# Softmax rows left unnormalised for the first six pairs of heads, and the output scaled by transposed reciprocals

## The chip, the cores and the metric

The kernel runs on one core of one Trainium2 chip. The metric is the device time in microseconds of one execution. TensorE (PE in the rows, PEld its weight loads), VectorE (DVE), ScalarE (ACT) and GpSimd (POOL) run side by side, each through its own list of instructions in order. SyncE (SP) issues the DMAs.

## The reference

Three stages follow one another: an attention with a threshold, a mixture of neighbouring tokens with a squared ReLU and a gate ("moe"), and a gated convolution ("moe2").

```
# 8 batches, 8 heads, 576 tokens, 64 per head
scores = q @ k.T / 8
thresh = max(scores, axis=-1) - tau
scores = where(scores >= thresh, scores, -1e9)
attn = exp(scores - max(scores))
attn = attn / (sum(attn) + 1e-9)
x = heads joined(attn @ v)                                # 8 x 576 x 512
xk = mu_k*x + (1-mu_k)*x_prev;  xr = mu_r*x + (1-mu_r)*x_prev
k = relu(xk @ w_k);  v = (k*k) @ w_v;  x = sigmoid(xr @ w_r) * v
gate = sigmoid(causal conv of 5 taps over x);  out = (gate * (x @ w_val)) @ w_out
```

## The kernel before

The attention goes through 32 pairs of heads (four pairs to a batch). A pair is nine chunks: chunks 0 to 7 are 128 query rows of one of the two heads in turn, and chunk 8 is the last 64 rows of both. The rows shown below and the prediction count pairs from the first to the thirty-second, nine chunks each.

One chunk passes through the engines so: TensorE forms the scores `s` in PSUM from `qkh` and its small remainder `kl` (four matmuls of 288 columns; eight in chunk 8; L409); VectorE takes their minimum (L419; the scores carry a minus sign); GpSimd adds tau to it (L422); ScalarE writes the exponentials into `p` (L432); VectorE multiplies them with the mask and sums the row into a column of the tile `sm` (L436); the sum is guarded with 1e-9 (L441, on GpSimd for the first 15 chunks, on VectorE after them) and inverted on VectorE (L446); GpSimd multiplies the 128x576 tile `p` with it (L449); TensorE transposes `p` in blocks of 128x128 into a PSUM bank `g` (L466), ScalarE copies these into `pt` (L477, L480, L485, L488). After chunks 3 and 8 TensorE multiplies `pt` with `v` (L515, L518) into a bank, and ScalarE copies that half of the pair's output into `x` (L525), whose rows are the two heads' 64 outputs and whose columns are tokens. Each pair also needs its inputs cast and split (`qkh` L356, L360 on ScalarE, remainders `kl` L364 on VectorE and L370 on GpSimd).

While the first pairs run, the float64 weights w_k and w_v come in as bits and are turned into a high and a low part, 16 pieces of 128x512 (tiles `wst` and `stage`): L264, L274, L304 on ScalarE, L267, L270 on VectorE, L277 on GpSimd, and the low part L307 on VectorE or GpSimd.

When the first batch's four pairs have left their `x`, the products of the moe stage begin (L551, 464 tokens a block, ten blocks, 192 matmuls of w_k and w_v to a block). They are mixed into the rest of the attention on TensorE. After the attention come the products with w_r, w_val and w_out, 1440 matmuls.

PSUM has eight banks. The scores hold two double banks, and a third (`s3`) for the first S3_CHUNKS chunks, if the chunk's number calls for it; after that the third's two banks join `g0` and `g1` as `g2` and `g3`, which transposes, outputs and products share.

The order on each engine isn't that of the code. Each step is recorded with an engine, a due time (its priority) and the buffers that it takes and frees (`acq`, `rel`); a planner then plays them through with estimated durations and emits them in the order it finds. Constants such as EARLY, MOE_LAG (how long after its batch a moe block is due) or MIX_AT shift those due times. An operation given as `{dve: .., pool: ..}` goes to whichever engine the planner finds free, as the low parts of weights do.

Of the kernel before, what the change touches and what calls it, by code (L numbers as in the profile page):

```python
# [8 lines left out]
F32 = mybir.dt.float32  # L9
# [5 lines left out]
ALU = mybir.AluOpType  # L15
# [10 lines left out]
PAD, TW = 4, 464  # L26
# [27 lines left out]
class Plan:  # L54
# [90 lines left out]

EARLY, QK_EARLY, T_LATE, EV_EARLY, AV_LATE = 0.7408, 0.3765, -0.2385, 2.6476, 0.0528
S3_CHUNKS = 48
MOE_LAG = 0.6411  # L150
MOE_STEP = 0.8064
KSTAGE = 4
KBUFS, XKBUFS = 10, 4
CVB = 3
GATES = {"a": 1, "b": 3}
XRS = {"a": 1, "b": 1}
MIX_EARLY, SIDE_EARLY = 1.1121, -0.2697
W_KEY, W_STEP = -0.5451, 2.6541
V_KEY, V_STEP = 1.365, -0.2017
R_AHEAD = 0  # L160
HOP = 240.0
VAL_LAG, OUT_LAG = 2.3457, 3.4035
LATE2, LOAD2, MIX2, CONV_LAG, THR_EARLY = -0.2908, 11.9577, 6.0432, 11.1059, 3.4422
MIX_AT = 332.7791
GUARD_POOL = 15
OUT_FETCH = 8.1497
# [6 lines left out]
def body(ctx, tc, qka, qkb, vp, w_k, w_v, w_r, w_val, w_out, conv_w, par, out):  # L173
    nc = tc.nc
    ctx.enter_context(tc.manual_schedule())
    plan = Plan()
    op = plan.op

    def dma(nbytes, fn, deps=(), prio=0.0, acq=(), rel=()):

        return op("dma", max(480, nbytes / 360), fn, deps, prio, acq, rel, lat=2000)
    tokens = plan.tokens
# [10 lines left out]
    ident = par_t[:, 0:128]  # L193
# [8 lines left out]
                            op0=ALU.mult, op1=ALU.add)  # L202
# [9 lines left out]
    g_s, tau_t = gs[:, 0:1], gs[:, 2:3]  # L212


    XBUFS, RAWS = 8, 2
# [27 lines left out]
    tokens.update(raw=RAWS, qk=4, kla=2, klb=2, v=2, p=3, pt=1, sm=4, s=2, s3=1, g0=1, g1=1,  # L243
                  x=XBUFS, xk=XKBUFS, xf=2, kh=0, cwst=KSTAGE, k2=2, vo=2, mm=2, cstage=1)
    BANKS = tuple(f"g{i}" for i in range(8))
    tokens.update({x: 0 for x in BANKS[2:]})
# [3 lines left out]
    by = {"dve": nc.vector, "pool": nc.gpsimd}  # L250
# [82 lines left out]
    x_t, x_done, x_kept = {}, {}, {}  # L333
    qk_t, kl_t, qk_done = {}, {}, {}
    v_t, v_done = {}, {}
    s_t, p_t, pt_t, sm_t, av_t, tps, tr_op, av_op = {}, {}, {}, {}, {}, {}, {}, {}

    def chain(kind, o):
        last[kind] = o
        return o  # L340
# [48 lines left out]
    def chunk(g):  # L389

        pi, c = seq[g]
        b, pp = pairs[pi]
        j, head = divmod(c, 2)
        at = g * PACE
        both = c == 8
        s_tok = "s3" if g < S3_CHUNKS and g % 3 == 2 else "s"


# [14 lines left out]
        o = op("pe", dur, lambda: qk(0), deps, at - QK_EARLY, acq=(s_tok,))  # L413
        o = chain("qk", op("pe", dur, lambda: qk(1), (o,), at - QK_EARLY, rel=("qk", "qk", "kla", "klb") if c == 8 else ()))
# [76 lines left out]
        o = op("pe", 440 * slow, lambda: tr((g, 0), [(k0 + i * 128, 128) for i in range(4)]), (nm, last.get("t")), lt,  # L491
               acq=(BANKS, "pt") if c in (0, 4) else (BANKS,))
# [5 lines left out]
        if head or c == 8:  # L498
            o = op("pe", 115, lambda: tr((g, 1), [(512, 128 if c < 8 else 64)]), (o,), lt, acq=(BANKS,), rel=("p",))
# [5 lines left out]
        if c in (3, 8):  # L505
            half = c // 8
            n = 256 + 64 * half

            def av():
                pt, ptl = pt_t[pi, half]  # L510
                v = v_t[pi]
                acc = av_t[pi, half] = bank(av_op[pi, half])
                for kc in range(4):
                    for h in range(2):
                        nc.tensor.matmul(acc[h * 64:h * 64 + 64, 0:n],  # L515
                                         lhsT=v[:, kc * 128 + h * 64:kc * 128 + h * 64 + 64],
                                         rhs=pt[:, h, kc, 0:n], start=(kc == 0), stop=False)
# [15 lines left out]
            chain("xe", x_done[b, pp])  # L533
            if half:
# [3 lines left out]
    half_evs = []  # L538

# [209 lines left out]
    def after_first():  # L749
# [5 lines left out]
               rel=BANKS[4:] + ("mm", "mm"))  # L755
# [213 lines left out]
```

## Time and profile before

| | before |
|---|---|
| median of 3 runs | 1294.17 us (1291.86 to 1294.76) |
| the profiled execution | 1293.29 us |
| its span, first to last instruction | 1291.2 us |
| busy: PE, DVE, ACT, POOL | 95%, 74%, 65%, 56% of the span |
| mean granted TensorE clock | 0.989 |

The shares are means over a start in which the attention runs alone, a long middle in which moe products fill TensorE, and an end of products only. 2.1 us of the profiled execution lie outside its span.

### The profile page before, as it was taken

What the parts mean: (1) busy time and instruction counts of PE and PEld (TensorE: products, weight loads), DVE (VectorE), ACT (ScalarE), POOL (GpSimd) and SP (SyncE); (2) the same over time, 40 slices, a digit from 0 to 9 for tenths busy, and PEclk for the clock granted to TensorE, in tenths of its full rate; (3) what the DMA queues carried; (4) which work ended last, traced back from release to release, by engine and by line L of the source; (5) the groups of instructions that cost most, each with busy time, mean ns of one, the idle gap of its engine ahead of it and who ended that gap; (6) DMA issues with size and microseconds to landing.
All of it is one profiled execution on the core that took longest, in us unless ns stands there. A gap on an engine that the chain in (4) does not pass through costs nothing.

```text
span 1291.2 us, 21070 instructions
## 1 busy us (share of the span) xinstructions
PE 1232.2 (95%) x7104; PEld 1041.5 (81%) x7104; DVE 959.2 (74%) x2086; ACT 835.4 (65%) x1608; POOL 724.9 (56%) x953
## 2 busy tenths in 40 slices
PE   5776999999999999999999999999999999999998
PEld 4555778887888887888888888888888888888897
DVE  7999998798888889779799697872433996665520
ACT  7877877777677667577687675662543876554432
POOL 6988766667665666547567456441203854553341
PEclk9889999999999999999999999999999999999999
DMA  7343232342322343223333212105105432230011
GB/s 243 124 129 114 93 99 88 107 138 92 130 83 80 115 124 113 82 85 118 115 105 111 82 61 74 54 11 190 53 15 193 139 118 89 92 110 36 30 48 70
DMA packets 51339, 127.57 MB, mean 99 GB/s; under 512 B 8608, under 2 KB 26144, under 8 KB 50464
## 3 DMA queue, kind: packets, MB, share of 16 engines
q1 hardware_dynamic: 51232, 126.23, 29.3%
q8 instruction: 57, 0.93, 0.3%
q14 instruction: 50, 0.41, 0.1%
HBM read 91.48 MB, written 34.73 MB: 98 GB/s over the span
## 4 chain that ended last, share of the span: by engine, by line
PE 70%; DVE 10%; ACT 7%; POOL 5%; issue 4%; DMA 4%; SPq 0%; DVEq 0%; POOLq 0%; ACTq 0%
PE g L551 43%; PE s L409 9%; PE g L515 8%; PE g L466 7%; PE g L518 3%; POOL p L449 2%; ACT p L432 1%; DVE sm L419 1%; DVE p L436 1%; DVE g L856 1%; POOL qkh L370 1%; ACT pt L477 1%; POOL sm L422 1%; DVE xf L608 1%; DMA xt<-x_d 1%
## 5 line engine op out<-in xcount | busy, mean ns | idle before, releaser
L449 POOL TENSOR_SCALAR p<-p,sm 128x576 f32<-128x576 f32 x288 | 237.0, 828 | 150.1 <-DVE sm L446 68.0
L432 ACT ACTIVATE p<-s,sm 128x576 f32<-128x576 f32 x288 | 212.8, 748 | 72.5 <-DVE sm L419 46.6
L436 DVE SCALAR_TENSOR_TENSOR p<-s,sm,p 128x576 f32<-128x576 f32 x288 | 231.1, 812 | 37.5 <-ACT p L432 23.0
L419 DVE TENSOR_REDUCE sm<-s 128x1 f32<-128x576 f32 x288 | 214.0, 749 | 55.4 <-PE s L409 54.0
L409 PE MATMUL s<-qkh 128*128 128x288 f32 x640 | 210.3, 343 | 23.6 <-DVE p L436 13.9
L466 PE MATMUL g<-par_t,p 128*128 128x128 f32 (+1 forms) x1312 | 191.4, 278 | 21.8 <-POOL p L449 8.5
L466 PEld LDWEIGHTS g<-par_t,p 128*128 128x128 f32 (+1 forms) x1312 | 157.3, 142 | 36.8 <-POOL p L449 14.9
L422 POOL TENSOR_SCALAR sm<-sm,gs 128x1 f32<-128x1 f32 x288 | 120.4, 420 | 114.6 <-DVE sm L419 64.4
L409 PE MATMUL s<-kl,qkh 128*128 128x288 f32 x640 | 183.5, 302 | 0.1
L477 ACT ACTIVATE pt<-g 128x512 f32<-128x512 f32 x256 | 147.9, 602 | 26.5 <-PE g L466 26.2
L409 PEld LDWEIGHTS s<-qkh 128*128 128x128 f32 x640 | 124.3, 194 | 39.3 <-DVE p L436 16.8
L515 PE MATMUL g<-pt,v 128*64 128x320 f32 (+1 forms) x1024 | 142.0, 420 | 5.0 <-ACT pt L480 3.5
L409 PEld LDWEIGHTS s<-kl,qkh 128*128 128x128 f32 x640 | 124.6, 195 | 5.0 <-DVE kl L364 0.7
L551 PE MATMUL g<-xkh,w_k_hi 128*128 128x464 f32 x320 | 123.9, 387 | 0.2 <-ACT pt L477 0.2
L551 PE MATMUL g<-kh,w_v_hi 128*128 128x464 f32 x320 | 123.2, 385 | 0.2 <-ACT pt L477 0.2
L551 PE MATMUL g<-kh,w_v_lo 128*128 128x464 f32 x320 | 119.1, 372 | 0.0
L551 PE MATMUL g<-xkh,w_k_lo 128*128 128x464 f32 x320 | 119.1, 372 | 0.0
L515 PEld LDWEIGHTS g<-pt,v 128*64 128x64 f32 x1024 | 69.2, 139 | 60.6 <-issue 12.8
L370 POOL TENSOR_TENSOR qkh<-raw,qkh 64x576 fp32r<-64x576 f32 x64 | 96.6, 1510 | 19.5 <-ACT qkh L360 7.4
L856 DVE SCALAR_TENSOR_TENSOR g<-y,cw_t,g 128x464 f32<-128x464 f32 x160 | 103.8, 699 | 4.3 <-ACT g L853 3.4
L627 POOL TENSOR_TENSOR xrl<-xf,xrh 128x464 fp32r<-128x464 f32 x40 | 51.6, 1304 | 89.8 <-ACT xrh L624 66.2
L888 POOL TENSOR_TENSOR gvl<-gate,gvh 128x464 fp32r<-128x464 f32 x40 | 48.5, 1212 | 91.8 <-ACT gvh L885 89.3
(99 smaller groups left out, 2605.5 us busy)
## 6 DMA issues: line engine op xcount, KB each, us to landing
raw<-in_qkb SPq DMA_DIRECT2D x32, 640.0 KB, 4.0
raw<-in_qka SPq DMA_DIRECT2D x32, 608.0 KB, 3.9
v<-in_vp SPq DMA_DIRECT2D x32, 320.0 KB, 3.2
x_d<-x SPq DMA_DIRECT2D x32, 290.0 KB, 3.9
v_d<-vo SPq DMA_DIRECT2D x40, 232.0 KB, 2.0
vt<-v_d SPq DMA_DIRECT2D x10, 928.0 KB, 4.8
wst<-in_w_k SPq DMA_DIRECT2D x8, 512.0 KB, 5.9
stage<-in_w_v SPq DMA_DIRECT2D x8, 512.0 KB, 3.8
```

Source lines behind the costliest of these rows:

```text
L370: nc.gpsimd.tensor_tensor(out=t["hi"][lo_rows, qs], in0=t["raw"][lo_rows, qs], in1=t["hi"][lo_rows, qs].bitcast(F32), op=ALU.subtract)
L409: nc.tensor.matmul(s_t[g][:, hh, 0:NT], lhsT=q, rhs=k, start=(i == 0), stop=(i == len(terms) - 1))
L419: nc.vector.tensor_reduce(out=sm[:, 0:1], in_=s_t[g][:, :, 0:NT], op=ALU.min, axis=AX.XY)
L422: nc.gpsimd.tensor_scalar(out=sm_t[g][:, 1:2], in0=sm_t[g][:, 0:1], scalar1=tau_t, scalar2=1.0, op0=ALU.add, op1=ALU.mult)
L432: nc.scalar.activation(out=view(), in_=s_t[g][:, :, 0:NT], func=AF.Exp, bias=sm_t[g][:, 0:1], scale=-1.0)
L436: nc.vector.scalar_tensor_tensor(out=view(), in0=s_t[g][:, :, 0:NT], scalar=sm[:, 1:2], in1=view(), op0=ALU.is_le, op1=ALU.mult, accum_out ...
L449: nc.gpsimd.tensor_scalar(out=view(), in0=view(), scalar1=sm_t[g][:, 3:4], scalar2=1.0, op0=ALU.mult, op1=ALU.mult)
L466: nc.tensor.transpose(ps[0:w, i * 128:(i + 1) * 128], in_=p_t[pi, j][:, p0:p0 + w], identity=ident)
L477: nc.scalar.activation(out=pt[:, head, :, q0:q0 + 128], in_=ps.rearrange("p (k q) -> p k q", k=4), func=AF.Copy)
L515: nc.tensor.matmul(acc[h * 64:h * 64 + 64, 0:n], lhsT=v[:, kc * 128 + h * 64:kc * 128 + h * 64 + 64], rhs=pt[:, h, kc, 0:n], start=(kc == ...
L551: nc.tensor.matmul(ps()[:, 0:TW], lhsT=W[w][wt][:, kc, m * 128:(m + 1) * 128].bitcast(F32R), rhs=a(at, kc), start=(i == 0 and x == 0), sto ...
L856: nc.vector.scalar_tensor_tensor(out=f["ps"], in0=t["y"][:, c, k:k + TW], scalar=cw[:, c, k:k + 1], in1=f["ps"], op0=ALU.mult, op1=ALU.add)
```

## The change

For the first six pairs (LATE_PAIRS) the guard, the reciprocal and the multiplication of `p` are left out of the chunk. The mask writes the row's sum into a column of a tile `ss` that serves a half pair (chunks 0 to 3, or 4 to 8), and frees `sm` itself; the transposes wait for the mask. Once in a half pair VectorE guards and inverts the four or five columns together, GpSimd copies each inverted column 64 times side by side into `rb`, TensorE transposes `rb` (two or three blocks of 128x128) into a PSUM bank, where now every row of a head holds the inverted sums along the tokens, and VectorE multiplies the half's `x` by it.

```
 late = pi < LATE_PAIRS
...
+                ss_t[pi, part] = ss_p.tile([128, 8], F32, name="ss", tag="ss")
+                to = ss_t[pi, part][:, slot:slot + 1]
...
+        if late:
+            nm = mk
+            masks.append(mk)
+        else:
+            gd = op({"dve": 70}, 0, guard, (mk,), e)
+            rc = op("dve", 76, recip, (gd,), e)
+            nm = op("pool", 790, norm, (rc,), e, rel=("sm",))
...
+                def widen():
+                    rb = r["rb"] = ss_p.tile([128, 3, 2, 64], F32, name="rb", tag="rb", bufs=1)
+                    nc.gpsimd.tensor_copy(out=rb[:, 0:2], in_=ss[:, 0:4]... .to_broadcast([128, 2, 2, 64]))
+                    if half:
+                        nc.gpsimd.tensor_copy(out=rb[:, 2]..., in_=ss[:, 4:5].to_broadcast([128, 128]))
+                def lay():
+                    ps = r["ps"] = bank(r["op"])
+                    for q in range(2 + half):
+                        nc.tensor.transpose(ps[:, q * 128:(q + 1) * 128], in_=r["rb"][:, q]..., identity=ident)
+                def scale():
+                    nc.vector.tensor_tensor(out=x[:, 0:256], in0=r["ps"][:, 0:256], in1=x[:, 0:256], op=ALU.mult)
+                    for h in (0, 64) if half else ():
+                        nc.vector.tensor_tensor(out=x[h:h + 64, 256:320], in0=r["ps"][h:h + 64, ...],
+                                                in1=x[h:h + 64, 256:320], op=ALU.mult)
```

The guards that stood on GpSimd go (GUARD_POOL), `x` has 7 buffers where it had 8, and all due times change with the table; of it, for example:

```
-S3_CHUNKS = 48
-MOE_LAG = 0.6411
+S3_CHUNKS = 40
+MOE_LAG = 0.3141
```

What the planner makes of it is seen in the order. First GpSimd, at the start of the first pair, before (L422 the threshold, L441 the guard, L449 the multiplication of `p`, L370 the remainder of q):

```order
L422 TENSOR_SCALAR sm_221<-sm_221,gs_90 128x1
L449 TENSOR_SCALAR p_189<-p_189,sm_175 128x576
L441 TENSOR_SCALAR sm_195<-sm_195 128x1
L441 TENSOR_SCALAR sm_202<-sm_202 128x1
L370 TENSOR_TENSOR qkh_228<-raw_183,qkh_228 64x576
L422 TENSOR_SCALAR sm_258<-sm_258,gs_90 128x1
L449 TENSOR_SCALAR p_189<-p_189,sm_195 128x576
```

And the same place of the change (L427 is the threshold, L566 the widening, L372 the remainder of q):

```order
L427 TENSOR_SCALAR sm_264<-sm_264,gs_90 128x1
L427 TENSOR_SCALAR sm_276<-sm_276,gs_90 128x1
L566 COPY rb_295<-ss_199 128x256
L427 TENSOR_SCALAR sm_290<-sm_290,gs_90 128x1
L372 TENSOR_TENSOR qkh_259<-raw_185,qkh_259 64x576
```

The large multiplications and the guards between the thresholds are gone, and one copy stands there for the half pair. Next VectorE of the change, from the inversion of the first half pair's sums (L561) to the scaling of its output (L580); L446 is the mask, L424 the minimum:

```order
L561 RECIPROCAL ss_199<-ss_199 128x4
L424 TENSOR_REDUCE sm_290<-s_272 128x1
L366 SCALAR_TENSOR_TENSOR kl_298<-raw_174,gs_90,qkh_207 128x576
L446 SCALAR_TENSOR_TENSOR p_288,ss_314<-s_229,sm_264,p_288 128x576
L309 TENSOR_TENSOR w_k_lo_145<-wst_152,w_k_hi_144 128x512
L446 SCALAR_TENSOR_TENSOR p_288,ss_314<-s_256,sm_276,p_288 128x576
L446 SCALAR_TENSOR_TENSOR p_319,ss_314<-s_272,sm_290,p_319 128x576
L366 SCALAR_TENSOR_TENSOR kl_337<-raw_185,gs_90,qkh_259 128x640
L424 TENSOR_REDUCE sm_352<-s_329 128x1
L269 TENSOR_SCALAR stage_164<-stage_164 128x512
L424 TENSOR_REDUCE sm_371<-s_344 128x1
L580 TENSOR_TENSOR x_332<-g0_361,x_332 128x256
```

Ten other instructions of VectorE stand between the two. Last TensorE, where the first moe products begin: before, in the sixth pair, four of them between scores,

```order
L466 MATMUL g0_1557<-par_t_83,p_1419 128x128
L551 MATMUL g1_1561<-xkh_656,w_k_hi_141 128x464
L551 MATMUL g1_1561<-xkh_656,w_k_lo_142 128x464
L551 MATMUL g1_1561<-xkh_869,w_k_hi_141 128x464
L551 MATMUL g1_1561<-xkh_869,w_k_lo_142 128x464
L409 MATMUL s_1571<-qkh_1284 128x288
```

and now, right behind the fifth pair's last scores and its transposed reciprocals (L575), a whole product of twelve (L607), of which these are the first:

```order
L575 MATMUL g1_1436<-par_t_83,rb_1366 128x128 x2
L481 MATMUL g3_1440<-par_t_83,p_1302 128x128 x4
L481 MATMUL g0_1449<-par_t_83,p_1302 128x128
L481 MATMUL g2_1452<-par_t_83,p_1401 128x128 x4
L607 MATMUL g1_1460<-xkh_589,w_k_hi_144 128x464
L607 MATMUL g1_1460<-xkh_589,w_k_lo_145 128x464
```

Counted in TensorE's order, 24 moe products stood ahead of the last scores of the sixth pair, and 56 do now; ahead of the last scores of all, 1428 and 1488. On VectorE, up to the mask of chunk 45 (the end of the fifth pair), 45 reciprocals and 30 guards are replaced by 10 and 10, 9 scalings of 128x256 and 8 of 64x64 are new, the subtractions of the low part of w_k go from 5 to 2 (on GpSimd from 3 to 6), and one piece of `stage` (L267, L270, and L277 on GpSimd) and one minimum stand later. On GpSimd 44 multiplications and 15 guards go up to there, and 15 copies come.

## Rows read from the trace of the kernel before

**Rows 1.** The page: TensorE's busy tenths in 40 slices of the span.
```profile
PE   5776999999999999999999999999999999999998
```
**Rows 2.** Busy time by stretch of the span; PEclk is the granted clock.
```profile
8.00:135.00 127.00, 95.59 (x555) 71.54 (x556) 120.21 (x262) 101.30 (x192) 111.15 (x147) 0.91 0.44 142
...
870.00:1291.00 421.00, 412.96 (x1982) 364.71 (x1980) 216.89 (x331) 206.84 (x386) 161.01 (x145) 1.00 0.26 91
```
**Rows 3.** Waits of PE from 8 to 135 us: total, times, longest.
```profile
PE s L409 <- DVE p L436: 8.0, 9, 2.8
PE g L466 <- POOL p L449: 7.1, 5, 2.2
PE g L466 <- ACT pt L477: 6.4, 7, 2.4
```
**Rows 4.** Stretches: masks on DVE (two records a chunk), then moe products on PE.
```profile
0.00:134.80 134.80, 36.21 (x90) 0.91 0.45 147
134.80:161.30 26.50, 7.41 (x19) 1.00 0.33 108
...
161.30:870.60 709.30, 331.96 (x1404) 1.00 0.29 94
```
**Rows 5.** Groups of instructions on DVE from 8 to 135 us.
```profile
L364 DVE SCALAR_TENSOR_TENSOR kl<-raw,gs,qkh 128x576 fp32r<-128x576 f32 (+1 forms) x13 | 14.2, 1092 | 3.9 <-ACT qkh L356 3.9
L270 DVE SCALAR_TENSOR_TENSOR wst<-wst 128x512 int32<-128x512 int32 x8 | 10.1, 1266 | 0.0
L307 DVE TENSOR_TENSOR w_k_lo<-wst,w_k_hi 128x512 fp32r<-128x512 f32 x5 | 9.1, 1822 | 0.0
L270 DVE SCALAR_TENSOR_TENSOR stage<-stage 128x512 int32<-128x512 int32 x6 | 7.2, 1195 | 0.0
L446 DVE RECIPROCAL sm<-sm 128x1 f32<-128x1 f32 x44 | 6.6, 153 | 1.6 <-POOL sm L441 1.4
```
**Rows 6.** Groups of instructions on POOL from 8 to 135 us.
```profile
L449 POOL TENSOR_SCALAR p<-p,sm 128x576 f32<-128x576 f32 x43 | 38.1, 891 | 5.3 <-DVE sm L441 2.8 <-DVE sm L446 2.5
...
L441 POOL TENSOR_SCALAR sm<-sm 128x1 f32<-128x1 f32 x15 | 4.0, 265 | 1.6 <-DVE p L436 0.5
```
**Rows 7.** Timeline from 118.6 us, DVE and then POOL: start, duration.
```profile
121.75 3.98 DVE L307 TENSOR_TENSOR w_k_lo<-wst,w_k_hi 128x512 fp32r<-128x512 f32 x1
...
121.18 0.70 POOL L422 TENSOR_SCALAR sm<-sm,gs 128x1 f32<-128x1 f32 x1
121.86 1.46 POOL L449 TENSOR_SCALAR p<-p,sm 128x576 f32<-128x576 f32 x2
123.30 0.65 POOL L602 TENSOR_SCALAR xf<-x,omu_t 128x464 f32<-128x464 f32 x1
123.92 1.26 POOL L277 TENSOR_TENSOR stage<-stage 128x512 int32<-128x512 int32 x1
```
**Rows 8.** Two lines of DVE over the whole span: duration min/median/max in ns.
```profile
L364 DVE SCALAR_TENSOR_TENSOR kl<-raw,gs,qkh x64: 794/1260/2510, 7.5 to 818.4; 128x576 fp32r<-128x576 f32 x32, 128x640 fp32r<-128x640 f32 x32
...
L270 DVE SCALAR_TENSOR_TENSOR stage<-stage x20: 674/690/1853, 19.4 to 671.0; 128x512 int32<-128x512 int32 x20
```
**Rows 9.** Groups by form, whole span: nearest to the new operations.
```profile
L879 DVE TENSOR_TENSOR gate<-g,gate 128x464 f32<-128x464 f32 x40 | 25.5, 637 | 47.3 <-PE g L551 46.8
...
L602 POOL TENSOR_SCALAR xf<-x,omu_t 128x232 f32<-128x232 f32 x16 | 9.2, 585 | 0.1
```
**Rows 10.** The chain that ended last, 139 to 156 us: start, us.
```profile
142.76 1.69 PE g L551 x8
144.46 2.31 PE g L515 x16
146.76 0.74 PE g L518 x2
...
147.76 0.44 PE g L466 x4
...
149.01 0.53 PE s L409 x4
```

More of the change, by code (lines that the diff above doesn't have):

```diff
@@ L144, in order @@
         return out
-EARLY, QK_EARLY, T_LATE, EV_EARLY, AV_LATE = 0.7408, 0.3765, -0.2385, 2.6476, 0.0528
-S3_CHUNKS = 48
-MOE_LAG = 0.6411
-MOE_STEP = 0.8064
+EARLY, QK_EARLY, T_LATE, EV_EARLY, AV_LATE = 1.149, 0.3839, -0.2831, 3.6059, 0.044
+S3_CHUNKS = 40
+MOE_LAG = 0.3141
+MOE_STEP = 0.8183
 KSTAGE = 4
+LATE_PAIRS = 6
 KBUFS, XKBUFS = 10, 4
@@ L156 @@
 XRS = {"a": 1, "b": 1}
-MIX_EARLY, SIDE_EARLY = 1.1121, -0.2697
-W_KEY, W_STEP = -0.5451, 2.6541
-V_KEY, V_STEP = 1.365, -0.2017
+MIX_EARLY, SIDE_EARLY = 2.0722, -0.1413
+W_KEY, W_STEP = -1.0263, 2.3326
+V_KEY, V_STEP = 1.7131, -0.1927
 R_AHEAD = 0
 HOP = 240.0
[L162 to L166, printed above, removed]
+VAL_LAG, OUT_LAG = 2.3927, 4.8834
+LATE2, LOAD2, MIX2, CONV_LAG, THR_EARLY = -0.1825, 14.8136, 3.0907, 7.4403, 4.8231
+MIX_AT = 410.1661
+OUT_FETCH = 8.4463
 SAME = {"dve": 130.0}
@@ L212, in body @@
     g_s, tau_t = gs[:, 0:1], gs[:, 2:3]
-    XBUFS, RAWS = 8, 2
+    XBUFS, RAWS = 7, 2
     moe = ExitStack()
@@ L228, in body @@
     sm_p = att.enter_context(tc.tile_pool(name="sm", bufs=4, side="right"))
+    ss_p = att.enter_context(tc.tile_pool(name="ss", bufs=3, side="right"))
     banks = {}
@@ L242, in body @@
     pool = {"s3": early.enter_context(tc.tile_pool(name="s3ps", bufs=1, space=PSUM, side="right"))}
-    tokens.update(raw=RAWS, qk=4, kla=2, klb=2, v=2, p=3, pt=1, sm=4, s=2, s3=1, g0=1, g1=1,
+    tokens.update(raw=RAWS, qk=4, kla=2, klb=2, v=2, p=3, pt=1, sm=4, ss=3, rb=1, s=2, s3=1, g0=1, g1=1,
                   x=XBUFS, xk=XKBUFS, xf=2, kh=0, cwst=KSTAGE, k2=2, vo=2, mm=2, cstage=1)
@@ L335, in body @@
     v_t, v_done = {}, {}
-    s_t, p_t, pt_t, sm_t, av_t, tps, tr_op, av_op = {}, {}, {}, {}, {}, {}, {}, {}
+    s_t, p_t, pt_t, sm_t, ss_t, av_t, tps, tr_op, av_op = {}, {}, {}, {}, {}, {}, {}, {}, {}
     def chain(kind, o):
@@ L395, in chunk @@
         both = c == 8
+        late = pi < LATE_PAIRS
+        part = min(c // 4, 1)
+        slot = 4 if both else 2 * head + j % 2
         s_tok = "s3" if g < S3_CHUNKS and g % 3 == 2 else "s"
@@ L435, in mask @@
             sm = sm_t[g]
+            to = sm[:, 2:3]
+            if late:
+                if c in (0, 4):
+                    ss_t[pi, part] = ss_p.tile([128, 8], F32, name="ss", tag="ss")
+                to = ss_t[pi, part][:, slot:slot + 1]
             nc.vector.scalar_tensor_tensor(out=view(), in0=s_t[g][:, :, 0:NT], scalar=sm[:, 1:2], in1=view(),
-                                           op0=ALU.is_le, op1=ALU.mult, accum_out=sm[:, 2:3])
+                                           op0=ALU.is_le, op1=ALU.mult, accum_out=to)
         def guard():
             sm = sm_t[g]
-            by[gd.eng].tensor_scalar(out=sm[:, 3:4], in0=sm[:, 2:3], scalar1=1e-9, scalar2=1.0,
+            nc.vector.tensor_scalar(out=sm[:, 3:4], in0=sm[:, 2:3], scalar1=1e-9, scalar2=1.0,
                                      op0=ALU.add, op1=ALU.mult)
@@ L454, in chunk @@
         e1 = chain("exp", op("act", 625, ex, (mx, last.get("exp")), e, acq=("p",) if head == 0 else ()))
-        mk = op("dve", 821, mask, (e1, th), e, rel=(s_tok,))
-        gd = op({"pool": 245} if g < GUARD_POOL else {"dve": 70}, 0, guard, (mk,), e)
-        rc = op("dve", 76, recip, (gd,), e)
+        mk = op("dve", 821, mask, (e1, th), e, acq=("ss",) if late and c in (0, 4) else (),
+                rel=(s_tok, "sm") if late else (s_tok,))
         if s_tok == "s3":
             last["s3"] = mk
-        nm = op("pool", 790, norm, (rc,), e, rel=("sm",))
+        if late:
+            nm = mk
[4 more added lines that the diff above has]
+            nm = op("pool", 790, norm, (rc,), e, rel=("sm",))
         def tr(key, blocks):
@@ L533, in chunk, with guard_all, recip_all @@
             chain("xe", x_done[b, pp])
+            if late:
+                n_s = 4 + half
+                r = {}
+                def guard_all():
+                    ss = ss_t[pi, half]
+                    nc.vector.tensor_scalar(out=ss[:, 0:n_s], in0=ss[:, 0:n_s], scalar1=1e-9, scalar2=1.0,
+                                            op0=ALU.add, op1=ALU.mult)
+                def recip_all():
+                    ss = ss_t[pi, half]
+                    nc.vector.reciprocal(ss[:, 0:n_s], ss[:, 0:n_s])
+                def widen():
+                    ss = ss_t[pi, half]
+                    rb = r["rb"] = ss_p.tile([128, 3, 2, 64], F32, name="rb", tag="rb", bufs=1)
+                    nc.gpsimd.tensor_copy(out=rb[:, 0:2], in_=ss[:, 0:4].rearrange("p (h q) -> p q h", h=2)
+                                          .unsqueeze(3).to_broadcast([128, 2, 2, 64]))
+                    if half:
+                        nc.gpsimd.tensor_copy(out=rb[:, 2].rearrange("p h q -> p (h q)"),
+                                              in_=ss[:, 4:5].to_broadcast([128, 128]))
+                def lay():
+                    ps = r["ps"] = bank(r["op"])
+                    for q in range(2 + half):
+                        nc.tensor.transpose(ps[:, q * 128:(q + 1) * 128],
+                                            in_=r["rb"][:, q].rearrange("p h q -> p (h q)"), identity=ident)
+                def scale():
+                    x = x_t[b, pp][:, 1 + PAD + half * 256:1 + PAD + half * 256 + n]
+                    nc.vector.tensor_tensor(out=x[:, 0:256], in0=r["ps"][:, 0:256], in1=x[:, 0:256], op=ALU.mult)
+                    for h in (0, 64) if half else ():
+                        nc.vector.tensor_tensor(out=x[h:h + 64, 256:320], in0=r["ps"][h:h + 64, 256 + h:320 + h],
+                                                in1=x[h:h + 64, 256:320], op=ALU.mult)
+                o = op("dve", 90, guard_all, masks, e)
+                o = op("dve", 160, recip_all, (o,), e)
+                masks.clear()
+                o = op("pool", 460 + 350 * half, widen, (o,), e, acq=("rb",), rel=("ss",))
+                o = r["op"] = op("pe", 110 * (2 + half), lay, (o, av_op[pi, half]), lt + AV_LATE, acq=(BANKS,), rel=("rb",))
+                x_done[b, pp] = chain("xe", op("dve", 340 + 280 * half, scale, (o, x_done[b, pp]), e, rel=(o,)))
             if half:
@@ L537, in chunk @@
                 x_kept[b, pp] = dma(296960, store_x, (x_done[b, pp],), at)
-    half_evs = []
+    half_evs, masks = [], []
     def mm3(ps, w, a, m, kcs):
```

## The prediction

> **What bounds the kernel now.** I read the page's slices first: TensorE is full in all but the first four and the last [rows 1]. What it loses it loses in the first 130 us, so I looked there by stretches. From 8 to 135 us TensorE is busy 95.6 of 127 us, VectorE 120.2 and GpSimd 111.2, which is 75%, 95% and 88%; the granted clock is 0.91, a mix of 2.4 and 1.2 GHz [rows 2]. So VectorE sets the pace there, with GpSimd close behind. TensorE's waits agree: 8.0 us for VectorE's mask, which frees a score buffer, 7.1 us for GpSimd's multiplication of `p`, 6.4 us for ScalarE's copies [rows 3]. The masks of the first five pairs (90 records, two a chunk) are done at 134.8 us, the sixth pair's at 161.3 us [rows 4].
>
> The next reading is why VectorE is so full. In that stretch its split of k (L364) takes 1092 ns in the mean and its bit operations on the weights (L270) 1266 and 1195 ns [rows 5], and over the whole span the same lines go down to 794 and 674 ns [rows 8]. One case shows what they wait for: a subtraction of 128x512 lasts 3.98 us, from 121.75 to 125.73, while GpSimd works without a gap from 121.18 to 125.18 through a threshold, two multiplications of `p`, a mix and an addition [rows 7]. VectorE's own work fits into what is left after the train. I read this as: VectorE's operations on two SBUF tensors stand still while GpSimd works.
>
> From 161.3 us on TensorE is the bound. An estimate of its work by the chain's pieces: four score matmuls 0.53 us, four transposes 0.44, eight products 1.69, the output of a second half 2.31 + 0.74 [rows 10]. A pair has 40 score matmuls (5.3 us), 41 transposes (4.5), and both halves of the output (3.05, and by columns 256/320 of it, 2.44): 15.3 us. A moe product is 0.211 us. Between 161.3 and 870.6 us lie 26 pairs and 1404 products [rows 4]: 398 + 296 = 694 of 709 us, 98%. Behind 870 us PE is busy 413 of 421 us [rows 2]. There a gain could only come out of the last few per cent, so what counts is how early TensorE fills, and how much of its work is done by then.
>
> **The change part by part, up to the end of the fifth pair, on VectorE.** All durations in the records overlap the next instruction by about 0.07 us, so I count a small instruction (153 ns, [rows 5]) at 0.07, not 0.15.
> - Removed: 45 reciprocals and 30 guards in that stretch, 75 x 0.07 = 5.2 us; three subtractions of w_k at the unhindered 0.69 (taken from L270, also 128x512 with two SBUF tensors, [rows 8]), 2.1 less overlap, 1.9; L270 of one piece of `stage` that stands later, 0.6. In all 7.7 us.
> - Added: 20 small ones, 1.4 us; 9 scalings of 256 columns and 8 of 64. The nearest row is L879, also PSUM times SBUF, 637 ns for 464 columns [rows 9]; between it and 153 ns for one column the line gives 0.42 and 0.22, less overlap 0.35 and 0.15: 4.4 us. In all 5.8 us.
> - Net: 1.9 us less.
> - The standing still. Over the unhindered durations VectorE loses 8 x 0.58 + 6 x 0.51 on L270, 5 x 1.13 on L307, 13 x 0.30 on L364: 17.2 us [rows 5, 8]. GpSimd loses 38.1 + 4.0 us of work [rows 6] and one addition (1.26), and gets 15 copies (0.59 each by the 232-column row, [rows 9]: 8.9) and three subtractions (1.26 each by the addition in [rows 7]: 3.8). Its 111.2 us become 80.5, in a stretch of some 118 us 68% where it was 88%. The three moved subtractions alone take 3.4 us of the loss with them, and the other 13.8 fall to 10.7 if the loss goes with GpSimd's share: 6.5 us less. If it goes with the length of trains, it falls more, since the multiplications were what closed the gaps. The ends are 0 and 17; I take 9, between the share and the trains, and nearer the share.
>
> [...] The 3.98 us row covers four groups of GpSimd work and speaks for whole trains [rows 7]. [...]
>
> So the fifth pair ends 1.9 + 9 = 10.9 us earlier, at 123.9.
>
> **The loop that is new.** After a half pair's last mask come guard, inversion, widening on GpSimd, transposes on TensorE, scaling on VectorE. The engines are in order, so whatever is early waits: behind the widening stand thresholds, behind the transposes of `rb` those of the next chunk, behind the scaling minima and masks. I price it at nothing, because ten other VectorE instructions stand between the inversion and the scaling in the order, of which three masks (0.80 each, [rows 4]), two splits of k and a subtraction alone are over 4.5 us, against about 0.6 + 0.3 us for widening and transposing plus whatever stands ahead in the two queues. If that cover is gone, each wait delays the pacing engine; a rival below. The transposes are no longer behind reciprocal and multiplication, so the 7.1 us of [rows 3] vanish; TensorE isn't the bound there, and I count nothing for it. The 30 added transposes are 0.11 us each; the five in the sixth pair count.
>
> **The sixth pair and the rest.** TensorE's order now has 56 products ahead of the sixth pair's last scores, 24 before. The pair is 15.3 + 11.8 (56 products, all in it) + 0.55 = 27.7 us of TensorE; at 98% 28.2 us, where it took 26.5 with only 20.4 us of work in it. VectorE was not far from full there either; its six more passes over the moe's hidden tiles, at the unhindered 0.69 us, still leave it within 28 us, with the reciprocals gone. So the sixth pair ends at 152.1 instead of 161.3, 9.2 us earlier, with 32 products (6.8 us; at 98% 6.9) done that were still to do. From there TensorE has the rest to do at the same fill: 16.1 us less in all. 1293.3 (profiled) less 16.1 is 1277.2; the median of the runs lies 0.9 above the profiled one, so I say 1278. For the later due times I count nothing: TensorE's list is 60 products ahead at the end of the attention, no hole in the order is visible, and at 98% there is little to win.
>
> With the standing still unchanged it is 9 us less gain, 1287; with all of it gone 8 us more, 1270. That is the forecast's own range.
>
> **The rivals.**
> - A gain that doesn't come: VectorE keeps its pace, because ScalarE (101 of 127 us, [rows 2]) and the chain through it limit the chunks as much. For it: the 6.4 us that PE waits for its copies. Against: VectorE is at 95%. Then only the 32 products count, less 1.7 us that the sixth pair is longer: 1294.2 - 5.2 = 1289.
> - A larger gain: trains on GpSimd go away altogether, the holes on TensorE close and its clock stays at 2.4 GHz where the mean was 0.91. All 17.2 us, 8 more than I took, and 4 from the chains that faster matmuls shorten (half of the 8.0 us for masks): 1278 - 12 = 1266.
> - Slower: the loop costs a bank. Until chunk 40 only `g0` and `g1` serve transposes and outputs, and `rb`'s transposes hold one of them until VectorE, behind two masks, has scaled: 0.80 + 0.80 + 0.42 = 2.0 us, in which the next transposes, and behind them the scores, stand in TensorE's queue, until VectorE has nothing to reduce. Twelve times 2.0 is 24 us, against 16.1: about 1302. It decides from 1.3 us per half pair. For it: PE waits seven times for such banks already [rows 3]. Against: three score buffers lie between TensorE and VectorE.
> - The gain is given back later: seven buffers of `x`, two score buffers from chunk 40 on and the shifted due times open holes in the middle, where 2% are lost now. Twice that loss, 15 us more, would bring the time to 1293, no change.
>
> **How the numbers follow.** Forecast 1270 to 1287: 0.55. Small gain 0.14; larger gain 0.10; given back 0.08; slower 0.13. A measurement of this kernel tells 0.2% (2.6 us) from no change. Faster is the first three, 0.79; same 0.08; slower 0.13. For eight times in ten the range takes the forecast, the small gain and part of the larger one and of the giving back: 1264 to 1291.
>
> **What would show it.** Right: the mask of chunk 45 near 124 us; L270, L307 and L364 near 0.7 to 0.9 us in that stretch, and GpSimd near two thirds busy; the first moe product some 13 us earlier, right behind that mask; waits on the scaling (its wait for the bank) and on `rb` under 3 us together; the stretch from the sixth pair on with the same fill. Wrong: VectorE's idle before the scaling or the masks, more than 1 us per half pair; TensorE waiting for banks before chunk 40; a middle below 97%.

## The result and the profile after

The changed kernel takes 1272.21 us (median of 3 runs, 1271.04 to 1272.87); the ratio to before is 0.9834, 95% interval 0.9818 to 0.985. That is 22 us less, inside the range on record and 6 us below the 1278 that was forecast. The profiled execution's span is 1270.4 us, 20.8 less, and the mean granted clock 0.999.

The page's tenths for TensorE, which answer [rows 1]:

```profile
PE   6888999999999999999999999999999999999998
```

The holes at the left are smaller; the rest looks the same in tenths. By stretches (columns as in [rows 2]: busy time of PE, PEld, DVE, ACT and POOL, then the granted clock):

```profile
8.00:121.70 113.70, 93.76 (x594) 70.94 (x595) 111.19 (x218) 98.51 (x191) 77.47 (x104) 0.98 0.45 153
121.70:152.30 30.60, 29.83 (x189) 24.59 (x188) 29.41 (x54) 24.74 (x51) 17.67 (x24) 1.00 0.36 115
152.30:864.20 711.90, 704.61 (x4444) 591.42 (x4443) 588.90 (x1435) 507.89 (x987) 437.88 (x636) 1.00 0.29 94
864.20:1270.40 406.20, 399.90 (x1913) 353.98 (x1911) 210.32 (x323) 199.50 (x379) 158.89 (x142) 1.00 0.26 93
```

GpSimd is busy 77.5 of 113.7 us, 68%, in place of 88%; VectorE 111.2 us, 98%, and still sets the pace. The borders are the ends of the 45th, the 54th and the last mask, as the masks by themselves show (two records a chunk, to be set beside [rows 4]):

```profile
0.00:121.70 121.70, 35.59 (x90) 0.99 0.46 157
121.70:152.30 30.60, 7.09 (x19) 1.00 0.36 115
152.30:864.20 711.90, 189.67 (x468) 1.00 0.29 94
```

So the fifth pair is done 13 us earlier (121.6 after 134.7), the sixth 9 us earlier (152.2 after 161.2), and by then TensorE has started 71 moe products where it had started 36. Twelve of the 71 stand ahead of the 45th mask; the first starts at 118.7 us, 20.5 us earlier than before. What VectorE did up to the 45th mask, by line, to be set beside [rows 5] (L366 is the split of k, L272 the bit operations, L309 the subtraction, L556 and L561 guard and inversion of a half pair, L580 and L582 the scaling):

```profile
L366 DVE SCALAR_TENSOR_TENSOR kl<-raw,gs,qkh 128x576 fp32r<-128x576 f32 (+1 forms) x12 | 12.6, 1047 | 4.1 <-ACT qkh L358 4.1
L272 DVE SCALAR_TENSOR_TENSOR wst<-wst 128x512 int32<-128x512 int32 x8 | 7.2, 895 | 0.0
L556 DVE TENSOR_SCALAR ss<-ss 128x4 f32<-128x4 f32 (+1 forms) x10 | 5.6, 558 | 0.1
L272 DVE SCALAR_TENSOR_TENSOR stage<-stage 128x512 int32<-128x512 int32 x5 | 4.9, 976 | 0.0
...
L580 DVE TENSOR_TENSOR x<-g,x 128x256 f32<-128x256 f32 x9 | 3.7, 411 | 0.2 <-ACT x L540 0.2
...
L309 DVE TENSOR_TENSOR w_k_lo<-wst,w_k_hi 128x512 fp32r<-128x512 f32 x2 | 2.5, 1247 | 0.3 <-ACT w_k_hi L306 0.3
L582 DVE TENSOR_TENSOR x<-g,x 64x64 f32<-64x64 f32 x8 | 1.7, 217 | 0.1
L561 DVE RECIPROCAL ss<-ss 128x4 f32<-128x4 f32 (+1 forms) x9 | 1.6, 174 | 0.1
```

The scaling waits for next to nothing (0.2 us in nine). TensorE's waits from 8 us to the 45th mask, beside [rows 3]:

```profile
PE g L481 <- ACT pt L492: 8.7, 14, 1.6
...
PE s L414 <- DVE p L446: 3.2, 5, 1.0
...
PE g L481 <- DVE x L580: 1.3, 2, 0.8
PE g L481 <- DVE x L582: 1.3, 1, 1.3
```

The 7.1 us for the multiplication of `p` are gone, those for the mask fell from 8.0 to 3.2, those for ScalarE's copies rose from 6.4 to 8.7, and the bank that the scaling holds costs 2.6 us in three waits. TensorE's largest single wait in both kernels, 8.4 us before and 8.3 now for the first cast of q and k, is not touched by the change.

### The profile page after: what moved, and what is told of

Same layout as the page of the kernel before. It is cut to its first block, busy times and chain, and to the rows that moved or that the text cites. A ratio compares the mean times of both kernels' runs of the same rounds, so it can differ in the third digit from the quotient of the medians.

```text
span 1270.4 us, 21004 instructions
## 1 busy us (share of the span) xinstructions
PE 1228.1 (97%) x7134; PEld 1040.9 (82%) x7134; DVE 941.2 (74%) x2033; ACT 834.2 (66%) x1608; POOL 693.5 (55%) x910
## 5 line engine op out<-in xcount | busy, mean ns | idle before, releaser
L459 POOL TENSOR_SCALAR p<-p,sm 128x576 f32<-128x576 f32 x234 | 195.9, 841 | 134.7 <-DVE sm L456 70.5
L424 DVE TENSOR_REDUCE sm<-s 128x1 f32<-128x576 f32 x288 | 213.6, 749 | 63.3 <-PE s L414 61.8
L446 DVE SCALAR_TENSOR_TENSOR p<-s,sm,p 128x576 f32<-128x576 f32 x288 | 230.4, 811 | 33.4 <-ACT p L437 21.3
L414 PE MATMUL s<-qkh 128*128 128x288 f32 x640 | 207.6, 339 | 13.7 <-ACT qkh L362 8.3
L427 POOL TENSOR_SCALAR sm<-sm,gs 128x1 f32<-128x1 f32 x288 | 119.2, 415 | 128.3 <-DVE sm L424 72.9
L607 PE MATMUL g<-xkh,w_k_hi 128*128 128x464 f32 x320 | 123.9, 387 | 0.4 <-DVE x L580 0.3
L607 PE MATMUL g<-kh,w_v_hi 128*128 128x464 f32 x320 | 123.4, 385 | 0.4 <-ACT pt L492 0.4
L607 PE MATMUL g<-kh,w_v_lo 128*128 128x464 f32 x320 | 119.9, 375 | 0.8 <-POOL w_v_lo L309 0.8
L607 PE MATMUL g<-xkh,w_k_lo 128*128 128x464 f32 x320 | 119.8, 374 | 0.0
L372 POOL TENSOR_TENSOR qkh<-raw,qkh 64x576 fp32r<-64x576 f32 x64 | 95.7, 1495 | 29.9 <-ACT qkh L362 14.5
```

The source lines that it names most:

```text
L372: nc.gpsimd.tensor_tensor(out=t["hi"][lo_rows, qs], in0=t["raw"][lo_rows, qs], in1=t["hi"][lo_rows, qs].bitcast(F32), op=ALU.subtract)
L414: nc.tensor.matmul(s_t[g][:, hh, 0:NT], lhsT=q, rhs=k, start=(i == 0), stop=(i == len(terms) - 1))
L424: nc.vector.tensor_reduce(out=sm[:, 0:1], in_=s_t[g][:, :, 0:NT], op=ALU.min, axis=AX.XY)
L427: nc.gpsimd.tensor_scalar(out=sm_t[g][:, 1:2], in0=sm_t[g][:, 0:1], scalar1=tau_t, scalar2=1.0, op0=ALU.add, op1=ALU.mult)
L459: nc.gpsimd.tensor_scalar(out=view(), in0=view(), scalar1=sm_t[g][:, 3:4], scalar2=1.0, op0=ALU.mult, op1=ALU.mult)
L607: nc.tensor.matmul(ps()[:, 0:TW], lhsT=W[w][wt][:, kc, m * 128:(m + 1) * 128].bitcast(F32R), rhs=a(at, kc), start=(i == 0 and x == 0), sto ...
```

## The experiments

Two theories to begin with. **A**: GpSimd's multiplications held VectorE up, and their absence makes the start of the attention shorter; the new due times only use it. **B**: the gain is that of the due times, which fill TensorE with products earlier. Beside them **C**: GpSimd's load doesn't matter, the chain from mask to transposes is shorter.

Each run's profile is read in the same two pieces: the end of the 45th mask (the fifth pair), and what follows it to the end of the span. "Products" are the moe products that TensorE has started by the end of the 54th mask. The two pieces are those of one profiled execution of each kernel, the medians those of three to twelve. The profiled execution lies within 2 us of its median but for the scaling only, where it took 1284.81 us, 4.8 above. The ratio is to executions of the kernel before taken beside each run, with medians of 1292.73 to 1294.17 us.

| run | 45th mask, us | behind it, us | products | median, us | ratio to before (95%) |
|---|---|---|---|---|---|
| before | 134.7 | 1156.5 | 36 | 1294.17 | |
| due times only | 132.5 | 1148.3 | 60 | 1281.47 | 0.9911 (0.9891 to 0.9931) |
| scaling only | 126.3 | 1156.7 | 16 | 1280.01 | 0.9905 (0.9877 to 0.9933) |
| changed kernel | 121.6 | 1148.8 | 71 | 1272.21 | 0.9834 (0.9818 to 0.985) |
| GpSimd loaded, multiplications | 128.4 | 1150.3 | 70 | 1281.44 | 0.9911 (0.9889 to 0.9934) |
| GpSimd loaded, zero fills | 138.1 | 1152.3 | 70 | 1291.55 | 0.9994 (0.9981 to 1.0007) |
| no loop | 118.0 | 1148.8 | 70 | 1269.95 | 0.982 (0.9803 to 0.9836) |
| no guard | 120.9 | 1149.3 | 71 | 1270.57 | 0.9821 (0.9806 to 0.9836) |
| four late pairs | 122.1 | 1148.6 | 69 | 1273.07 | 0.9846 (0.983 to 0.9862) |
| eight late pairs | 122.4 | 1148.0 | 71 | 1272.67 | 0.9841 (0.9826 to 0.9856) |
| changed, old MOE_LAG, MOE_STEP | 122.9 | 1156.3 | 53 | 1283.09 | 0.9923 (0.9902 to 0.9943) |
| scaling only, new MOE_LAG, MOE_STEP | 124.0 | 1166.3 | 20 | 1291.55 | 0.9984 (0.9968 to 1.0001) |

**Due times only.** The new table, no late pair. The first 15 guards, on GpSimd before, are on VectorE here, and `x` has 7 buffers, as in every run of this section.

```
-LATE_PAIRS = 6
+LATE_PAIRS = 0
```

Expected: 

> The new due times with no late pair: every chunk keeps its guard, reciprocal and multiplication on GpSimd. Theory A (the multiplication's absence on GpSimd sets VectorE free; due times only use it): the mask of chunk 45 stays near 134 us, L272 and L366 on VectorE near 1.2 and 1.1 us, and of the gain only the products that stand earlier are left (52 ahead of the sixth pair's last scores where before has 24, 28 x 0.21 = 5.9 us): 1284 to 1290. Theory B (the due times bring the gain, products filling TensorE earlier): 1272 to 1278.

Measured: 1281.47 us, below A's range and above B's. The 45th mask moved by only 2.2 us, as A has it, but what follows fell by 8.2 us, more than the products that stand earlier explain. And A was wrong on VectorE's lines: the bit operations and subtractions got faster although GpSimd stayed 86% busy up to there, while the split of k and the mixing of tokens (L664, 1153 ns before) got slower.

```profile
8.00:132.60 124.60, 101.00 (x578) 74.18 (x578) 118.15 (x276) 101.67 (x194) 106.61 (x133) 0.92 0.45 145
```

```profile
L366 DVE SCALAR_TENSOR_TENSOR kl<-raw,gs,qkh 128x576 fp32r<-128x576 f32 (+1 forms) x13 | 16.5, 1271 | 4.0 <-ACT qkh L358 4.0
L272 DVE SCALAR_TENSOR_TENSOR wst<-wst 128x512 int32<-128x512 int32 x8 | 7.4, 921 | 0.0
...
L664 DVE SCALAR_TENSOR_TENSOR xf<-x,par_t,xf 128x464 f32<-128x464 f32 x4 | 6.4, 1588 | 0.5 <-POOL xf L658 0.5
...
L309 DVE TENSOR_TENSOR w_k_lo<-wst,w_k_hi 128x512 fp32r<-128x512 f32 x5 | 4.6, 928 | 0.3 <-ACT w_k_hi L306 0.2
```

The first of these two blocks is the stretch, the second VectorE's groups in it. The subtractions took 1822 ns before and 928 here, the bit operations on `wst` 1266 and 921, with the same multiplications on GpSimd. By the prediction's way of counting (13 x 0.48 on L366, 8 x 0.23 + 5 x 0.26 on L272, 5 x 0.24 on L309) VectorE stands still for 10.5 us, where before it was 17.2. That count leaves out the other lines, and most of the difference has only moved to them: over all lines it is 19.7 us, where before it was 21.8 (the table behind the loaded runs). So with this load on GpSimd the order decides more which instructions stand still than for how long in all.

**Scaling only.** The late scaling with the due times of before, so the constants of the diff's first part stay.

```
+LATE_PAIRS = 6
```

Expected: 

> The late scaling with the due times of before. Theory A: the fifth pair's last mask near 123 us, 11 us earlier than before; products are not placed earlier (12 ahead of the sixth pair's last scores), so some of that is lost again: 1278 to 1287. Theory B: no gain without the due times, 1290 or more.

Measured: 1280.01 us, in A's range. The 45th mask comes 8.4 us earlier, not the 11 that A had, and what follows is what it was (1156.7 after 1156.5 us). In the profiles the two halves of the change are thus almost separate: the scaling shortens the start (8.4 us alone, 10.9 on top of the due times), the due times shorten the rest (8.2 alone, 7.9 on top of the scaling). By the medians, 13.0 us for the scaling alone and 11.6 for the due times alone make 24.6, where both together give 22.0. Where the other 4.8 us of the scaling's median lie, its profile of a longer execution can't show.

**GpSimd loaded again.** The changed kernel with its order, and work on GpSimd that nobody waits for, behind each late chunk's threshold: first multiplications of a scratch tile, then zero fills of it.

```
             nc.gpsimd.tensor_scalar(out=sm_t[g][:, 1:2], ...)
+            if late:
+                for h in (0, 1):
+                    nc.gpsimd.tensor_scalar(out=idle_t[:, h, 0:144], in0=idle_t[:, h, 0:144], scalar1=1.0, ...)
```
```
+            if late:
+                for h in (0, 1, 2):
+                    nc.gpsimd.memset(idle_t, 0.0)
```

Expected of the multiplications: 

> The changed kernel, and behind each late chunk's threshold GpSimd multiplies a scratch tile by one in two instructions (128x144 each, SBUF to SBUF), which nobody waits for: GpSimd's load is back, the chain of a chunk stays short; nothing else in the order changes. Theory A: the fifth pair's last mask back to 130 to 135 us, L272 above 1.1 us, total 1280 to 1286. Theory C (the gain is the shorter chain from mask to transposes, not GpSimd's load): the mask stays within 2 us of 121.5 us and the total within 3 us of 1272.

Expected of the fills: 

> As the run with scratch multiplications, but GpSimd fills the scratch tile with zeros (three times 128x288) behind each late chunk's threshold: busy, without reading SBUF. If VectorE stands still only for GpSimd work that reads SBUF, L272 and L366 stay near 0.9 and 1.05 us, the fifth pair's last mask stays within 3 us of 121.5 and the total near 1272 to 1275. If GpSimd being busy is enough, or if late thresholds are what counts, it goes as the run with multiplications, 1278 to 1286, in proportion to the busy time added.

Measured: the multiplications put 30.3 us on GpSimd up to the 45th mask, which comes 6.8 us later; the total is 1281.44 us. That is A's range for the total, short of its 130 us for the mask, and not C's. The place on VectorE was not the one expected, though: L272 (L275 in this run) hardly changed; the split of k (L369) and one-input operations with a scalar did, the guards of the sums (L563, 779 ns where the changed kernel has 558) and the shifts of the weights (L272 in this run, 900 ns; L269 in the changed kernel, 585).

```profile
L369 DVE SCALAR_TENSOR_TENSOR kl<-raw,gs,qkh 128x576 fp32r<-128x576 f32 (+1 forms) x12 | 15.2, 1270 | 3.9 <-ACT qkh L361 3.9
...
L563 DVE TENSOR_SCALAR ss<-ss 128x4 f32<-128x4 f32 (+1 forms) x10 | 7.8, 779 | 0.1
L272 DVE TENSOR_SCALAR wst<-wst 128x512 int32<-128x512 int32 x8 | 7.1, 900 | 0.0
```

The fills put 45.7 us on it and cost 16.5 us up to the mask and 19 in the total, far outside what was expected of work that reads nothing. VectorE's rows show another way: its masks (L451 in this run) sat idle for 11.0 us, 8.6 of it for thresholds that stood behind the fills in GpSimd's queue, while L274, the bit operations, stayed as short as in the changed kernel.

```profile
L451 DVE SCALAR_TENSOR_TENSOR p<-s,sm,p 128x576 f32<-128x576 f32 x45 | 36.3, 813 | 11.0 <-POOL sm L429 8.6 <-POOL idle L433 0.9 <-ACT ptl L505 0.9
...
L274 DVE SCALAR_TENSOR_TENSOR wst<-wst 128x512 int32<-128x512 int32 x8 | 6.2, 773 | 0.0
```

So load on GpSimd costs the start in two ways: operations of VectorE that stand still beside GpSimd's work, and, when its queue is full (118.5 of 130.2 us here), late thresholds. The Trainium skill says in "SBUF — State Buffer", section "Who interferes with whom", that GpSimd work that only writes doesn't hold up VectorE's two-input operations; the 773 ns agree, the split of k (1290 ns in this run, with GpSimd's other reads also there) doesn't decide it.

What the runs make of VectorE as a whole, from 8 us to the 45th mask: standing still is here the sum over all its operations whose tensors lie in SBUF, each record less the shortest record of its operation and shape in any run, an estimate from the traces.

| run | GpSimd busy | VectorE idle, us | VectorE stands still, us |
|---|---|---|---|
| before | 88% | 6.8 | 21.8 |
| due times only | 86% | 6.5 | 19.7 |
| scaling only | 68% | 3.3 | 19.7 |
| changed kernel | 68% | 2.5 | 15.1 |
| GpSimd loaded, multiplications | 85% | 3.4 | 21.1 |
| GpSimd loaded, zero fills | 91% | 16.8 | 15.7 |

In the order of the changed kernel, reading load on GpSimd brings back 6.0 us of standing still, nearly all of the 6.8 by which the mask is later, and the fills bring back 0.6: 14.3 of the 16.5 us that they cost up to the mask are idle time. In the order of before, GpSimd at 68% takes off only 2.1 us; the 8.4 us of the scaling alone are these, 3.5 us of idle time, and work that is no longer on VectorE, the five subtractions of w_k among it. So GpSimd's load counts, but how much of it turns into standing still depends on the order, and no run here shows why.

**No loop; no guard.** The changed kernel without widening, transposes and scaling (`lay` and `scale` go like `widen`, and the six pairs' output stays unnormalised); and without the guard alone. The order of the rest stays.

```
-                o = op("pool", 460 + 350 * half, widen, ...)
+                o = op("pool", 460 + 350 * half, lambda: None, ...)
...
```
```
-                o = op("dve", 90, guard_all, masks, e)
+                o = op("dve", 90, lambda: None, masks, e)
```

Expected without the loop: 

> The changed kernel without widening, transposes of the reciprocals and scaling (the six pairs' output stays unnormalised; guard and reciprocal stay); the order of all else is the same. If the loop is hidden as priced (5.8 us of VectorE's work in the first five pairs, no waits), the fifth pair's last mask comes 3 to 6 us earlier and the total is 3 to 6 us below the changed kernel. Rival (banks and queues wait for the loop): 10 us or more below it.

Expected without the guard: 

> The changed kernel without the guard instruction on the row sums of the late pairs (1e-9 isn't added to sums that are at least 1); all else in the same order. In the changed kernel's trace these ten guards took 0.51 us in the mean and one of them 2.29 us. If that is standing still for GpSimd's work, 3 to 5 us of VectorE's time go and the total falls by 2 to 5 us; if the wait only moves on to the next such instruction, the total stays within 1.5 us.

Measured: without the loop the 45th mask comes 3.6 us earlier and the span is 3.6 us shorter (the medians, 1269.95 and 1272.21, are 2.3 us apart, less than the 3 to 6 expected, with overlapping intervals). The loop costs about its work on VectorE; the 10 us of the rival are not there. Without the guard, 0.7 us to the mask and 1270.57 us, 1.6 us less and not told apart from the changed kernel: the 5.6 us of the guards' row were mostly a wait that went on to other instructions (the bit operations on `stage` took 1179 ns, 976 with the guards).

**Four and eight late pairs.**

Expected of four: 

> Four late pairs where the change has six. The fifth pair is still paced by VectorE: with nine multiplications back on GpSimd its end comes 1 to 3 us later, 1273 to 1277. If only the first pairs matter (weights are split there), no change within 1.5 us.

Expected of eight: 

> Eight late pairs. From the sixth pair on TensorE is the bound, and ten more transposes cost it 1.1 us while the shorter chain gains nothing: 1271 to 1275, no difference that can be told. If VectorE still holds up pairs seven and eight, 1267 to 1270.

Measured: 1273.07 and 1272.67 us, both no different from six. The fifth pair's multiplications, back in the run with four, cost 0.5 us to the mask. Four late pairs are enough; fewer were not run. That it is because TensorE has no products there and the weights are split is argued, not shown.

**Two constants swapped.** MOE_LAG and MOE_STEP alone, in both directions.

```
-MOE_LAG = 0.3141
-MOE_STEP = 0.8183
+MOE_LAG = 0.6411
+MOE_STEP = 0.8064
```

Expected of the changed kernel with the old ones: 

> The changed kernel with MOE_LAG and MOE_STEP of before (0.6411, 0.8064), all else as changed. In the runs so far the new due times shortened what follows the fifth pair's last score by 6.7 us. If that is the two constants' doing (products due earlier), that stretch grows back from 1153.5 us by 4 to 7 us, the fifth pair's end stays near 117 us, and the total is 1276 to 1279. If it lies in the other due times, the total stays within 2 us of 1272.

Expected of the old table with the new ones: 

> The late scaling with the due times of before, but MOE_LAG and MOE_STEP new (0.3141, 0.8183). If the two constants carry the later gain, what follows the fifth pair's last score falls from 1161.2 us to 1154 to 1157 and the total to 1274 to 1277. If not, it stays near 1280.

Measured: the old ones in the changed kernel lengthen what follows the 45th mask by 7.5 us, nearly all of the due times' later gain, and the total is 1283.09 us, above the range. Behind the sixth pair TensorE is idle for 20.9 us there, 13.6 in the changed kernel. The new ones in the old table don't bring it: what follows grows to 1166.3 us. TensorE then waits in the middle for VectorE's masks and ScalarE's copies, here between 124 and 870 us,

```profile
PE s L414 <- DVE p L446: 6.3, 7, 2.7
PE g L530 <- ACT pt L495: 3.3, 4, 1.3
PE g L481 <- ACT pt L492: 3.0, 6, 1.4
PE g L481 <- POOL p L459: 2.2, 1, 2.2
```

where the changed kernel has 1.8 us for the mask. Part of the loss may be the clock: from 148 to 883 us 0.99 were granted, 1.00 in the changed kernel. So the two constants are needed for the later gain, and the other due times that fit them (EARLY, EV_EARLY, the mixes) as well; which of these, no run here tells.

So of the 20.8 us by which the span is shorter, 13.1 lie in the start, where A's standing still is half of the gain and the order has a part in it, and 7.7 lie behind it and are the due times', as B has it. C by itself would have left the mask where it was in the loaded run.

No version beat the changed kernel by more than the intervals.

## Why the prediction was right, and where not

- **What bounds the start.** Right: VectorE was 95% busy and is 98% busy. The 45th mask was foreseen at 123.9 and came at 121.6 us, but two errors cancel in part there (standing still and idle, below). The first product came 20.5 us earlier and ahead of that mask, not some 13 and behind it.
- **GpSimd's load.** Foreseen 68% busy up to there, measured 68%. The copies took 0.50 us (L566), foreseen at 0.59.
- **VectorE's added work.** The scalings took 411 and 217 ns, foreseen from the line between two rows at 0.42 and 0.22. The loop was priced at its work without waits; the run without it shows 3.6 us for widening, transposes and scaling, where 4.4 us were counted for the scaling.
- **The standing still.** By the same count (12 x 0.25 on L366, 8 x 0.21 + 5 x 0.29 on L272, 2 x 0.56 on L309) 7.2 us are left of 17.2; foreseen were 8.2. But the count has three lines only, and the others rose. Over all lines it fell from 21.8 to 15.1 us, 6.7, where the sum took 9. New, and not foreseen, is that the guards stand still: 0.56 us each in place of 0.15, 4 us. The prediction put all of it on the missing multiplications, and neither they nor the due times alone take off more than 2.1 us. Of the 0.7 to 0.9 us that it asked for as a sign, only the bit operations on `wst` came to the edge (0.90); those on `stage` took 0.98, L309 1.25 and L366 1.05.
- **Idle on VectorE.** Counted as nothing; it fell from 6.8 us [rows 2] to 2.5 in the start. The guards on GpSimd had stopped VectorE for 1.4 us and the multiplications for 1.2, which is gone; the waits for GpSimd's part of the mixing (1.0 us) and for the exponentials (1.8 us, now 0.8) went or got shorter. The 13.1 us are 6.7 less standing still, 2.1 less work (1.9 foreseen) and 4.3 less idle. Masks and minima before, then the masks after:

```profile
L436 DVE SCALAR_TENSOR_TENSOR p<-s,sm,p 128x576 f32<-128x576 f32 x45 | 35.9, 809 | 3.4 <-ACT p L432 1.8 <-POOL p L449 0.6 <-POOL sm L422 0.5
L419 DVE TENSOR_REDUCE sm<-s 128x1 f32<-128x576 f32 x46 | 33.9, 746 | 0.6 <-POOL p L449 0.6
```
```profile
L446 DVE SCALAR_TENSOR_TENSOR p<-s,sm,p 128x576 f32<-128x576 f32 x45 | 35.3, 805 | 1.1 <-ACT p L437 0.8 <-POOL sm L427 0.2
```

- **The sixth pair.** Foreseen to end at 152.1 us and ended at 152.2, but by two errors: it began 2.3 us earlier and took 30.7 us, not 28.2. It held 59 products, not 56. The pair counted as TensorE's work at 98%; TensorE was 29.8 us busy in it and VectorE 29.4, so the rows don't tell which paced it. With the old MOE_LAG and MOE_STEP it held 41 products and took 27.0 us, 0.2 us less for each product that was missing, as it would be if TensorE paced it.
- **The rest.** This is the step that was mis-sized: "For the later due times I count nothing", and with it "at the same fill". Behind the 54th mask lie 1118.1 us where there were 1130.0, 11.9 less. The step gave 6.9 us for the products done earlier; by the trace 35 more are started, 7.4 us. The rest is holes that closed: TensorE's idle time behind the 54th mask fell from 18.3 to 13.6 us, and its waits for masks there from 5.9 to 1.8. Before and then after, each with the stretch and the wait for masks in it:

```profile
161.20:1291.20 1130.00, 1111.72 (x6390) 950.10 (x6390) 813.72 (x1761) 709.83 (x1371) 592.36 (x774) 1.00 0.28 93
PE s L409 <- DVE p L436: 5.9, 12, 1.2
```
```profile
152.30:1270.40 1118.10, 1104.52 (x6355) 945.41 (x6353) 799.22 (x1757) 707.38 (x1365) 596.77 (x778) 1.00 0.28 94
PE s L414 <- DVE p L446: 1.8, 4, 1.1
```

The idle time is 13.3 us with the due times only, 16.9 with the scaling only, and 20.9 with the two old constants in the changed kernel. So the later gain is the due times'.

- **The total.** It came within 6 us of the forecast partly by luck: in the profiled execution the start gave 2.2 us more than foreseen and what lies behind the sixth pair 5.0 more, and the sixth pair took 2.5 us longer.
- **The rivals.** The small gain didn't come: VectorE did speed up. The slower one, a bank held by the loop until it delays VectorE, did leave a trace, 2.6 us of TensorE's waits in place of the 1.3 us per half pair from which it decides. Of the larger gain, the clock did rise (0.98 in the start, 0.91 before) and the waits for masks fell by 4.8 us; how much of that is the clock's own doing no run here tells. The scaling alone had 8.4 of the 13.1 us with 0.93 granted up to the mask. Nothing was given back later: in the middle TensorE was busy for 704.6 of 711.9 us, 99%.

## What to carry to other kernels

Where two engines disturb each other, look for the instructions whose durations differ from their minimum, and count the sum of that difference over the stretch that they pace: here 22 us of 127, of which 7 could be had. Count over all lines: on three of them alone it looked like 10 of 17, and a third of that had moved to others. Taking a full-width pass off the neighbour and doing it later on a much smaller tile paid here only in the stretch in which VectorE, which that neighbour holds up, sets the pace: four pairs were enough, and eight bought nothing. And a table of due times is part of such a change: with the old table the scaling gave 13 us of the 22, and two of the new constants put into that table gave nearly all of it away.

## What was not expected of the hardware

A VectorE operation on five numbers a row stood still for 2.1 us. VectorE's and then GpSimd's timeline of the changed kernel:

```profile
74.27 2.29 DVE L556 TENSOR_SCALAR ss<-ss 128x5 f32<-128x5 f32 x1
76.47 0.74 DVE L424 TENSOR_REDUCE sm<-s 128x1 f32<-128x576 f32 x1
```
```profile
73.64 1.66 POOL L372 TENSOR_TENSOR qkh<-raw,qkh 64x576 fp32r<-64x576 f32 x1
75.25 1.27 POOL L279 TENSOR_TENSOR wst<-wst 128x512 int32<-128x512 int32 x1
```

It has one input, takes 151 ns at the line's shortest, began while GpSimd ran a subtraction and ended at 76.56 us, right after GpSimd's next instruction (76.52): two GpSimd instructions, not one, as in [rows 7] it was a whole train of five. The minimum behind it, which reads PSUM and writes one column, took its usual 0.74 us. The Trainium skill, "SBUF — State Buffer", section "Who interferes with whom", has such scalar operations among those that can take the port pair that VectorE shares with GpSimd, and says that the later one waits until the other instruction is over; the first agrees with this row, the second is exceeded in both cases, where the wait lasts until GpSimd's queue leaves a gap.

These two are the longest waits of their traces and not the usual ones. One of the others, from the trace before, VectorE and then GpSimd:

```profile
46.57 1.80 DVE L270 SCALAR_TENSOR_TENSOR wst<-wst 128x512 int32<-128x512 int32 x1
```
```profile
46.54 1.29 POOL L307 TENSOR_TENSOR w_v_lo<-stage,w_v_hi 128x512 fp32r<-128x512 f32 x1
47.80 1.19 POOL L449 TENSOR_SCALAR p<-p,sm 128x576 f32<-128x576 f32 x1
```

It ended at 48.37 us, 0.54 us behind the one subtraction (47.83), while GpSimd's next instruction was already running. In that trace ten operations up to 140 us stood still for over 0.7 us; eight of them ended so, 0.5 to 0.8 us behind a single GpSimd instruction, and two behind a train. So the prediction's reading of whole trains, taken from one case, holds for the longest waits and not for most.
